# Copies of values bound behind the selections of turned probabilities, in attention followed by a feed-forward block

## The chip, the cores and the metric

The kernel runs on one core of one Trainium2 chip. The metric is the device time of one execution in microseconds (us). Before the change three runs took 711.4, 712.26 and 714.54 us, median 712.26. One more execution was profiled; the rows below are from it.

## The reference

Input are q, k and v of shape 4 x 8 x 768 x 64 (batch, heads, positions, head size), and two weights, 512 x 2048 and 2048 x 512. All is fp32.

```
scores = q @ k^T / sqrt(64)
keep   = (key < 4) or (0 <= query - key < 128)        # sinks, or a sliding window
a      = softmax over the kept keys
x      = (a @ v), heads side by side: 3072 x 512
h      = x @ w_in                                      # 3072 x 2048
g      = h * erf(softplus(h))
out    = g @ w_out                                     # 3072 x 512
```

## The kernel before

The 3072 positions are worked on in 12 groups of 256. Attention goes in 48 steps (s = 0 to 47): a step is one pair of heads of one group, so four steps make a group. The feed-forward block goes through each group in 16 blocks of 128 hidden units, taken in pairs; a pair bears the number m of its first block (h_54 is a hidden pair, g_55 its activations).

A step s from 15 on runs like this:

- `load` fetches k, q and v of the step into SBUF (DMAs issued by SyncE: L232, L241).
- `prep` turns k and q with a VectorE transpose (L345); `kcopy` (L328) and a small copy (L358) on GpSimd complete the keys, kq.
- `score` multiplies them on TensorE (L404, tile ps); VectorE merges the two window halves and takes the maximum (L417, L422), ScalarE takes the exponential (L426).
- `norm` divides by the sums on VectorE (L433 to L456). `ptrans` transposes in blocks (L469, L470) and writes the result to DRAM (L472); `pread` reads it back so that the probabilities are turned (L498, tile pa).
- `phalf` and `halves` run on GpSimd. Copies make the tile pz (L509, L513), then four selections at L522 keep one triangle each: two write pz from pa, and the last two write pa in place.
- `dup` copies the values v of the step into the tile vz, in two halves (L321 and L323), on GpSimd too.
- `av`, on TensorE (L563), multiplies pa with v and pz with vz. It needs the last selection of the step, and both copies. `xfin` (L582, L583) splits the result into a high and a low part for the feed-forward block.

In `core`, the av of step s - 2 stands just ahead of the scores of step s on TensorE. The feed-forward block uses L771 for the hidden products (24 matmuls of 256 columns a pair), ScalarE and VectorE for the activation (L784 to L793), L800 on VectorE for the high half of g and L801 on GpSimd for its low half, and L816 to L818 for the projection (12 matmuls of 512 columns a pair).

What sets the order. The program gives its pieces out in rounds (`plan`, `attn`), each with a priority (`at`, table `O`). A scheduler then sets the instructions of each engine in an order by these priorities and by when it expects their inputs; each engine runs its list strictly in that order. `follow(prev, ins)` binds an instruction behind another without a semaphore. In the plan `phalf(s - 1)` is given out one round ahead of `dup(s)`:

```
plan.setdefault(pos(s) + 5, []).append(("phalf", phalf, s))
plan.setdefault(pos(s) + 2, []).append(("dup", dup, s))      # pos(s) = 4 s - 12
```

but nothing binds the two, and `dup(s)` only needs its values to have landed, so the scheduler sets it where GpSimd would otherwise wait.

Of the kernel before, what the change touches and what calls it, by code (L numbers as in the profile page):

```python
# [45 lines left out]
TT = 15  # L46
# [16 lines left out]
def kernel(  # L63
# [11 lines left out]
    nc = tc.nc  # L75
# [62 lines left out]
    def fast_path():  # L138
        with ExitStack() as st:
# [52 lines left out]
            vz = pers.tile([P, 2, 2, H, D], F32, name="vz")  # L192
# [10 lines left out]
            mark = {}  # L203
# [3 lines left out]
            lo, hi = slice(0, HP), slice(HP, P)  # L207
# [109 lines left out]
            def dup(s):  # L317

                g, c = divmod(s, NPAIR)
                t, cs = stp[s]["v"], slice(2 * c, 2 * c + 2)  # L320
                nc.gpsimd.tensor_copy(vz[lo, 0, :, cs], t[lo, 1:])  # L321
                x = t[hi, 1:2].broadcast_to([HP, 2, 2, D]) if g % GPB == 0 else t[hi, :2]
                nc.gpsimd.tensor_copy(vz[hi, 1, :, cs], x)  # L323

            def kcopy(s):

# [3 lines left out]
            def follow(prev, ins):  # L330

                if prev is not None:
                    tc.add_manual_dep(
                        ins.ins, prev.ins.name,
                        mybir.DependencyInfo(mybir.DependencyClass.NoSync, mybir.DependencyReason.DATA), reason="order",
                    )
                return ins
# [123 lines left out]
            def ptrans(s):  # L461
# [27 lines left out]
                if i0:  # L489
                    nc.scalar.copy(pz[lo, :, 0, lo], tp[lo, :, 0, lo])  # L490
                halves(pa, pz, i0)

            def pread(s, last):
# [7 lines left out]
            def phalf(s):  # L501

                d = stp[s]
                pa, pz = d["pa"], work.tile([P, 2, 2, P], F32, tag="pz", bufs=AL, name=f"pz_{s}")
                d["pz"] = pz
                i0 = int(g_of(s) % GPB == 0)
                if i0:
                    nc.gpsimd.memset(pz[hi, :, 0, hi], 0.0)
                    nc.gpsimd.tensor_copy(pz[lo, :, 0, lo], pa[lo, :, 0, lo])  # L509
                for hf in (lo, hi):  # L510
                    other = hi if hf == lo else lo
                    y = d["pa5"][hf, 4, other].rearrange("p (a b t) -> p a b t", a=1, b=1)
                    nc.gpsimd.tensor_copy(pz[hf, :, :, other], y.broadcast_to([HP, 2, 2, HP]))  # L513
                halves(pa, pz, i0)

            def halves(pa, pz, i0):

                for hf in (lo, hi):
                    x = pa[hf, :, i0:, hf]
                    old, new = (1, ALU.is_gt), (-1, ALU.is_ge)  # L520
                    for out, (sg, op) in zip((pz[hf, :, i0:, hf], x), (new, old) if hf == lo else (old, new)):
                        nc.gpsimd.affine_select(  # L522
                            out=out, in_=x, pattern=[[0, 2], [0, 2 - i0], [-sg, HP]], compare_op=op, fill=0.0, base=0,
                            channel_multiplier=sg,
                        )
# [64 lines left out]
            def pos(s):  # L590

                return s if s < NE else 3 * s - 6 if s < 2 * NPAIR else 4 * s - 12

            plan = {}
            for s in range(NSTEP + AL):
                if s < NSTEP:
                    for what, fn, a in (
                        ("prep", prep, max(4, s - 1) if NE <= s < 2 * NPAIR else pos(s) - 3), ("norm", norm, pos(s) + 1 + (s == 1)), ("ptrans", ptrans, pos(s) + 2),
                        ("load", load, pos(s) - 4),
                    ):  # L600
                        if what == "load":
                            if s < 2 * NPAIR:
                                continue
                            plan.setdefault(a, []).append(("load", load_v, s))
                            a -= 1
                            if s >= TT + 2:
                                plan.setdefault(a - 2, []).append(("load", lambda s: load(s, "k"), s))
                                fn = load_q
                        plan.setdefault(max(a, 0 if what == "prep" else -1), []).append((what, fn, s))
                    if s >= TT:  # L610
                        if s + 2 >= NSTEP:
                            plan.setdefault(pos(s) + 3, []).append(("pread", lambda s: pread(s, mark["d", s]), s))
                        plan.setdefault(pos(s) + 5, []).append(("phalf", phalf, s))
                    if s >= 2 * NPAIR:
                        plan.setdefault(pos(s) + 2, []).append(("dup", dup, s))
                    if s // NPAIR % GPB < GPB - 1:
                        plan.setdefault(pos(s) + (2 if s < NE else 1), []).append(("kcopy", kcopy, s))
                plan.setdefault(pos(s), []).append(("core", core, s))
                if s < 2 * NPAIR:
                    x = pos(s) + (3 if s < NE else 5)  # L620
# [22 lines left out]
            for n in range(32):  # L643
                x = n - 16
# [326 lines left out]
```

## Time and profile before

| | before |
|---|---|
| median of 3 runs | 712.26 us |
| profiled execution | 710.78 us, its span 708.8 us |
| granted TensorE clock | 0.992 of full speed |
| busy: TensorE, its weight loads | 681.0 us (96%), 564.1 us |
| busy: VectorE, ScalarE, GpSimd | 550.0, 494.0, 297.8 us |
| TensorE idle for GpSimd (L522; L801) | 5.2 us in 6 places; 1.5 us in 4 |
| GpSimd idle for values (L321) | 21.5 us in 12 places |

The span is the time from the first to the last instruction that the profile shows; the execution's own time lies 2 us above it. Busy times overlap between engines, so they don't add up to the span. An idle time stands with the instruction that ended it and with what it waited for.

### The profile page before, as it was taken

Reading aid. Unit: us, or ns where it says so; the run is one execution under the profiler, and the core shown is the slowest. Engines: PE = TensorE matmul, PEld = TensorE weight load, DVE = VectorE, ACT = ScalarE, POOL = GpSimd, SP = SyncE. Lnnn points to the kernel's source line nnn. Section 1 sums busy time; section 2 is a strip of 40 time slices with the busy share of each in tenths; the row PEclk is TensorE's granted clock in tenths of the full one; section 3 lists DMA queues with packets and bytes.
Section 4 is the critical chain, followed back from the end, with each engine's and each line's share of the span. In section 5 each row is a group of like instructions: output and inputs, shape, how many; then the busy total and the mean of one; then the engine's idle time right before and its main releaser. Section 6 shows DMA issues by size and latency. Waiting matters only on the chain. (4 is left out here: it accounts for less than half of the span.)

```text
span 708.8 us, 16156 instructions
## 1 busy us (share of the span) xinstructions
PE 681.0 (96%) x5515; PEld 564.1 (80%) x5515; DVE 550.0 (78%) x1473; ACT 494.0 (70%) x1157; POOL 297.8 (42%) x501
## 2 busy tenths in 40 slices
PE   6789999999999999899999999999999999999997
PEld 3566566687888888788788888888888888889895
DVE  6979998787889889788898588788798687754352
ACT  4777777986984867476677586686578567586572
POOL 3512410234445545554555455455464337342221
PEclk9989999999999999999999999999999999999999
DMA  7999410202216454653564354453553543220001
GB/s 174 296 325 318 177 31 17 63 16 50 63 35 121 108 113 94 139 102 73 123 119 83 71 122 82 99 120 75 119 103 78 101 95 71 44 68 1 30 1 35
DMA packets 246858, 70.10 MB, mean 99 GB/s; under 512 B 214704, under 2 KB 238896, under 8 KB 246768
## 3 DMA queue, kind: packets, MB, share of 16 engines
q1 hardware_dynamic: 246208, 68.92, 41.8%
q8 instruction: 46, 0.75, 0.4%
q14 instruction: 44, 0.36, 0.2%
q10 hardware_dynamic: 560, 0.07, 0.1%
HBM read 50.27 MB, written 18.42 MB: 97 GB/s over the span
## 5 line engine op out<-in xcount | busy, mean ns | idle before, releaser
L771 PE MATMUL h<-xh,wt 128*128 128x256 f32 x1408 | 271.2, 283 | 1.2 <-DVE u L793 1.2
L771 PEld LDWEIGHTS h<-xh,wt 128*128 128x128 f32 x1408 | 223.4, 188 | 15.6 <-issue 7.8
L771 PE MATMUL h<-xl,wt 128*128 128x256 f32 x704 | 197.0, 280 | 0.3 <-DVE xl L583 0.3
L801 POOL TENSOR_TENSOR g<-u,g 128x512 fp32r<-128x512 f32 x84 | 113.6, 1353 | 176.4 <-DVE g L800 161.5
L789 ACT ACTIVATE u<-r 128x512 f32<-128x512 f32 x288 | 163.3, 623 | 20.4 <-DMA out_dram<-ot 5.5
L793 DVE SCALAR_TENSOR_TENSOR u<-u,u 128x512 f32<-128x512 f32 x168 | 136.2, 811 | 14.5 <-ACT u L789 1.4
L771 PEld LDWEIGHTS h<-xl,wt 128*128 128x128 f32 x704 | 132.4, 188 | 7.0 <-issue 2.8
L816 PE MATMUL o<-wt,g 128*128 128x512 f32 x336 | 133.2, 396 | 0.7 <-DVE g L800 0.6
L817 PE MATMUL o<-wt,g 128*128 128x512 f32 x336 | 132.2, 393 | 0.0
L818 PE MATMUL o<-wt,g 128*128 128x512 f32 x336 | 129.4, 396 | 1.7 <-POOL g L801 1.5
L426 ACT ACTIVATE pst<-pst,neg 128x144 f32<-128x144 f32 x192 | 77.4, 405 | 65.3 <-DVE neg L422 65.2
L793 DVE SCALAR_TENSOR_TENSOR u<-u,h 128x512 f32<-128x512 f32 x84 | 56.7, 675 | 50.6 <-ACT u L789 46.3
L784 ACT ACTIVATE r<-h 128x512 f32<-128x512 f32 x96 | 56.9, 593 | 45.3 <-PE h L771 34.4
L522 POOL TENSOR_SCALAR_AFFINE_SELECT pz<-pa 64x256 f32<-64x256 f32 (+1 forms) x96 | 47.5, 495 | 67.3 <-ACT pa L484 66.0
L816 PEld LDWEIGHTS o<-wt,g 128*128 128x128 f32 x336 | 63.1, 188 | 14.5 <-ACT u L789 1.3
L818 PEld LDWEIGHTS o<-wt,g 128*128 128x128 f32 x336 | 61.8, 188 | 15.9 <-POOL g L801 3.0
L817 PEld LDWEIGHTS o<-wt,g 128*128 128x128 f32 x336 | 63.1, 188 | 10.3 <-issue 0.3
L786 ACT ACTIVATE r<-r 128x512 f32<-128x512 f32 x96 | 60.6, 631 | 2.7
L785 ACT ACTIVATE r<-r 128x512 f32<-128x512 f32 x96 | 60.6, 632 | 2.5
L800 DVE CAST g<-u 128x512 fp32r<-128x512 f32 x84 | 37.5, 447 | 25.0 <-PE o L818 21.5
L513 POOL COPY pz<-pa 64x256 f32<-64x256 f32 x66 | 31.9, 484 | 56.3 <-DMA pa<-pd 55.5
L522 POOL TENSOR_SCALAR_AFFINE_SELECT pa<-pa 64x256 f32<-64x256 f32 (+1 forms) x96 | 47.7, 497 | 4.9
(99 smaller groups left out, 915.1 us busy)
## 6 DMA issues: line engine op xcount, KB each, us to landing
pd<-turn SPq DMA_DIRECT2D x33, 320.0 KB, 2.6
pa<-pd SPq DMA_DIRECT2D x132, 80.0 KB, 2.6
ws<-in_moe_w_in_dram SPq DMA_DIRECT2D x16, 512.0 KB, 6.0
ws<-in_moe_w_out_dram SPq DMA_DIRECT2D x16, 512.0 KB, 8.6
out_dram<-ot SPq DMA_DIRECT2D x24, 256.0 KB, 2.4
v<-in_v_dram SPq DMA_DIRECT2D x56, 96.0 KB, 2.5
kq<-in_k_dram SPq DMA_DIRECT2D x144, 32.0 KB, 2.0
kq<-in_q_dram SPq DMA_DIRECT2D x144, 32.0 KB, 2.2
```

The lines of the kernel that those rows point to most:

```text
L426: mark["e", s] = nc.scalar.activation(y, y, AF.Exp, bias=d["neg"][:, i, h : h + 1], scale=-1.0, accum_out=d["sum"][:, i, h : h + 1])
L522: nc.gpsimd.affine_select(out=out, in_=x, pattern=[[0, 2], [0, 2 - i0], [-sg, HP]], compare_op=op, fill=0.0, base=0, channel_multiplier=sg,)
L771: last = nc.tensor.matmul(o, wt[NC * j + c][:, p, fs], xt[e][:, c, :], start=(m == 0), stop=(m == len(ops) - 1))
L784: nc.scalar.activation(r, h, AF.Tanh, bias=b_t, scale=0.5)
L785: nc.scalar.activation(r, r, AF.Square, bias=b_v, scale=-0.5)
L786: nc.scalar.activation(r, r, AF.Square, bias=b_r)
L789: sq = nc.scalar.activation(u, r, AF.Square, bias=b_a[i], scale=CS)
L793: pr = nc.vector.scalar_tensor_tensor(out=acc, in0=u, scalar=CC[i] * CS**2, in1=x, op0=ALU.add, op1=ALU.mult)
L801: nc.gpsimd.tensor_tensor(gl, acc, gh.bitcast(F32), op=ALU.subtract)
L816: behind(nc.tensor.matmul(o, gh[:, ws], wt[16 + f][:, 0, :], start=(f == 0), stop=False))
L817: nc.tensor.matmul(o, gh[:, ws], wt[16 + f][:, 1, :], start=False, stop=False)
L818: nc.tensor.matmul(o, gl[:, ws], wt[16 + f][:, 0, :], start=False, stop=(f == NF - 1))
```

## The change

Two lines bind the copies of `dup`, for steps over TT = 15, behind `mark["half"]`, and `halves` puts its latest selection there. When `dup(s)` is given out, the latest `halves` is that of step s - 1, so the copies of step s stand behind the last selection of step s - 1 on GpSimd. The bond is of the order alone: no instruction and no semaphore wait is added.

```
 def dup(s):
     g, c = divmod(s, NPAIR)
     t, cs = stp[s]["v"], slice(2 * c, 2 * c + 2)
-    nc.gpsimd.tensor_copy(vz[lo, 0, :, cs], t[lo, 1:])
+    behind = mark["half"] if s > TT else None
+    follow(behind, nc.gpsimd.tensor_copy(vz[lo, 0, :, cs], t[lo, 1:]))
     x = t[hi, 1:2].broadcast_to([HP, 2, 2, D]) if g % GPB == 0 else t[hi, :2]
-    nc.gpsimd.tensor_copy(vz[hi, 1, :, cs], x)
+    follow(behind, nc.gpsimd.tensor_copy(vz[hi, 1, :, cs], x))
...
 def halves(pa, pz, i0):
...
-            nc.gpsimd.affine_select(
+            mark["half"] = nc.gpsimd.affine_select(
                 out=out, in_=x, pattern=[[0, 2], [0, 2 - i0], [-sg, HP]], compare_op=op, fill=0.0, base=0,
```

Lines from 322 on have a number higher by one in the changed kernel (L522 is L523, L321 is L322). The scheduler makes a new order of every engine. GpSimd, at the selections of step 22; the number after a tile's name is the step, v_24 are the values of step 24. Before:

```order
L522 AFFINE_SELECT pz_22_3878<-pa_22_3740 64x4x64
L513 COPY pz_22_3878<-pa_22_3740 64x4x64
L522 AFFINE_SELECT pz_22_3878<-pa_22_3740 64x4x64
L522 AFFINE_SELECT pa_22_3740<-pa_22_3740 64x4x64
L321 COPY vz_131<-v_24_3846 64x2x128
L323 COPY vz_131<-v_24_3846 64x2x128
L522 AFFINE_SELECT pa_22_3740<-pa_22_3740 64x4x64
L358 COPY kq_130<-kq_130 128x3x16
```

And in the changed kernel:

```order
L523 AFFINE_SELECT pz_22_3878<-pa_22_3740 64x4x64
L514 COPY pz_22_3878<-pa_22_3740 64x4x64
L523 AFFINE_SELECT pz_22_3878<-pa_22_3740 64x4x64
L523 AFFINE_SELECT pa_22_3740<-pa_22_3740 64x4x64 x2
L322 COPY vz_131<-v_23_3654 64x2x128
L324 COPY vz_131<-v_23_3654 64x2x128
L359 COPY kq_130<-kq_130 128x3x16
```

The two selections of pa now stand together, and the copies behind them are those of step 23, not 24.

TensorE, around av of step 17. Before, the hidden pair h_54 (24 matmuls, just above this piece), the 12 projections of g_49 and four of g_51 stand ahead of it; o_3 are the outputs of group 3:

```order
L816 MATMUL o_3_0_3008<-wt_17_2026,g_49_2862 128x512
L817 MATMUL o_3_0_3008<-wt_17_2026,g_49_2862 128x512
L818 MATMUL o_3_0_3008<-wt_17_2026,g_49_2862 128x512
L816 MATMUL o_3_1_3009<-wt_17_2026,g_49_2862 128x512
L817 MATMUL o_3_1_3009<-wt_17_2026,g_49_2862 128x512
L818 MATMUL o_3_1_3009<-wt_17_2026,g_49_2862 128x512
L816 MATMUL o_3_0_3008<-wt_18_2068,g_51_2985 128x512
L817 MATMUL o_3_0_3008<-wt_18_2068,g_51_2985 128x512
L816 MATMUL o_3_1_3009<-wt_18_2068,g_51_2985 128x512
L817 MATMUL o_3_1_3009<-wt_18_2068,g_51_2985 128x512
L563 MATMUL av_17_3071<-pa_17_2798,v_17_2548 64x128 x2
```

In the changed kernel the same av stands right behind the projections of g_47:

```order
L818 MATMUL o_2_1_2276<-wt_31_1975,g_47_2794 128x512
L819 MATMUL o_2_1_2276<-wt_31_1975,g_47_2794 128x512
L564 MATMUL av_17_3071<-pa_17_2798,v_17_2548 64x128 x2
L564 MATMUL av_17_3071<-pa_17_2798,v_17_2548 64x64 x4
L564 MATMUL av_17_3071<-pz_17_2946,vz_131 64x64 x8
L405 MATMUL ps_19_3088<-kq_130 64x208 x2
L405 MATMUL ps_19_3088<-kq_130 64x224 x2
L405 MATMUL ps_19_3088<-kq_130 64x208 x2
L405 MATMUL ps_19_3088<-kq_130 64x224 x2
L817 MATMUL o_3_0_3008<-wt_16_2023,g_49_2862 128x512
L818 MATMUL o_3_0_3008<-wt_16_2023,g_49_2862 128x512
L819 MATMUL o_3_0_3008<-wt_16_2023,g_49_2862 128x512
```

The projections of g_49 and h_54 have moved behind av and the scores of step 19.

The same count of feed-forward matmuls that change sides was made for the other steps: ahead of av of step 16, 11 projections of g_47 have moved behind; ahead of the scores of step 17, four of g_45; ahead of av of step 18, 33 hidden products and 8 projections, taken from where it stood before. From step 24 on av stands where it stood, or later: by up to two hidden pairs and two dozen projections at step 43.

## Rows read from the trace of the kernel before

**Rows 1.** The page, busy time of each engine (share of the span) and instructions.

```profile
PE 681.0 (96%) x5515; PEld 564.1 (80%) x5515; DVE 550.0 (78%) x1473; ACT 494.0 (70%) x1157; POOL 297.8 (42%) x501
```

**Rows 2.** Stages: window, us, busy time of each engine, clock, DMA.

```profile
0.00:50.00 50.00, 37.14 (x290) 25.84 (x291) 39.87 (x146) 33.18 (x100) 18.45 (x40) 0.92 0.93 256
...
400.00:450.00 50.00, 50.00 (x433) 43.65 (x430) 41.88 (x115) 36.87 (x86) 23.97 (x35) 1.00 0.46 97
```

**Rows 3.** Waits of TensorE, whole span: us in total, times, longest.

```profile
PE av L563 <- POOL pa L522: 5.2, 6, 1.9
...
PE o L818 <- POOL g L801: 1.5, 4, 0.6
PE h L771 <- DVE u L793: 1.2, 3, 0.5
```

**Rows 4.** Timeline of TensorE, instructions it idled before: start, us, instruction, [idle].

```profile
280.57 0.67 PE L563 MATMUL av<-pa,v 128*64 128x128 f32 x12 [0.24 <-POOL pa L522]
292.95 0.74 PE L818 MATMUL o<-wt,g 128*128 128x512 f32 x2 [0.56 <-POOL g L801]
301.95 0.67 PE L563 MATMUL av<-pa,v 128*64 128x128 f32 x12 [1.95 <-POOL pa L522]
...
352.73 0.34 PE L563 MATMUL av<-pa,v 128*64 128x64 f32 x4 [1.03 <-POOL pa L522]
```

**Rows 5.** Timeline of GpSimd, selections of step 22 and copies between them.

```profile
299.51 0.42 POOL L522 TENSOR_SCALAR_AFFINE_SELECT pa<-pa 64x256 f32<-64x256 f32 x1
299.88 0.84 POOL L321 COPY vz<-v 64x256 f32<-64x256 f32 x1
300.76 0.77 POOL L323 COPY vz<-v 64x256 f32<-64x256 f32 x1
301.48 0.42 POOL L522 TENSOR_SCALAR_AFFINE_SELECT pa<-pa 64x256 f32<-64x256 f32 x1
```

**Rows 6.** Timeline of GpSimd, copies and last selections of steps 17 and 18.

```profile
241.85 0.39 POOL L321 COPY vz<-v 64x256 f32<-64x256 f32 x1
242.28 0.77 POOL L323 COPY vz<-v 64x256 f32<-64x256 f32 x1
243.01 0.60 POOL L522 TENSOR_SCALAR_AFFINE_SELECT pa<-pa 64x256 f32<-64x256 f32 x1
...
255.43 0.39 POOL L321 COPY vz<-v 64x256 f32<-64x256 f32 x1
...
256.21 0.42 POOL L522 TENSOR_SCALAR_AFFINE_SELECT pa<-pa 64x256 f32<-64x256 f32 x1
```

**Rows 7.** Timeline of TensorE: 18 projections, hidden products, av of steps 17 and 18.

```profile
231.58 0.39 PE L816 MATMUL o<-wt,g 128*128 128x512 f32 x1
...
235.47 0.40 PE L818 MATMUL o<-wt,g 128*128 128x512 f32 x1
...
238.00 0.28 PE L771 MATMUL h<-xl,wt 128*128 128x256 f32 x1
...
243.23 0.28 PE L771 MATMUL h<-xh,wt 128*128 128x256 f32 x1
...
247.10 0.67 PE L563 MATMUL av<-pa,v 128*64 128x128 f32 x12
...
257.76 0.67 PE L563 MATMUL av<-pa,v 128*64 128x128 f32 x12
```

**Rows 8.** Timeline of VectorE beside the copies of step 22.

```profile
299.64 1.63 DVE L793 SCALAR_TENSOR_TENSOR u<-u,u 128x512 f32<-128x512 f32 x2
```

**Rows 9.** Idle time of GpSimd before L321: until what, us, times.

```profile
  DMA v<-in_v_dram: 21.5, 12
```

**Rows 10.** Timelines of GpSimd and TensorE, last selection and av of step 30.

```profile
397.99 0.42 POOL L522 TENSOR_SCALAR_AFFINE_SELECT pa<-pa 64x256 f32<-64x256 f32 x1
...
405.51 0.67 PE L563 MATMUL av<-pa,v 128*64 128x128 f32 x12
```

More of the change, by code (lines that the diff above doesn't have):

```diff
@@ L320, in dup @@
                 t, cs = stp[s]["v"], slice(2 * c, 2 * c + 2)
-                nc.gpsimd.tensor_copy(vz[lo, 0, :, cs], t[lo, 1:])
+                behind = mark["half"] if s > TT else None
+                follow(behind, nc.gpsimd.tensor_copy(vz[lo, 0, :, cs], t[lo, 1:]))
                 x = t[hi, 1:2].broadcast_to([HP, 2, 2, D]) if g % GPB == 0 else t[hi, :2]
-                nc.gpsimd.tensor_copy(vz[hi, 1, :, cs], x)
+                follow(behind, nc.gpsimd.tensor_copy(vz[hi, 1, :, cs], x))
             def kcopy(s):
@@ L521, in halves @@
                     for out, (sg, op) in zip((pz[hf, :, i0:, hf], x), (new, old) if hf == lo else (old, new)):
-                        nc.gpsimd.affine_select(
+                        mark["half"] = nc.gpsimd.affine_select(
                             out=out, in_=x, pattern=[[0, 2], [0, 2 - i0], [-sg, HP]], compare_op=op, fill=0.0, base=0,
```

## The prediction, made before the changed kernel was run

> **What bounds the kernel now.** I read the page first, then the table by stage, then TensorE's waits, then the timelines of TensorE and GpSimd around those waits. The page puts TensorE at 681.0 us of the 708.8 us span; GpSimd, which the change touches, is busy for 297.8 [rows 1]. So an instruction of GpSimd costs time only where TensorE waits for it. By stage TensorE is idle for 12.9 us in the first 50 us, before any moved copy, and not at all from 400 to 450 [rows 2]. What TensorE owes to GpSimd is small: the products of probabilities and values (I call them av, with the step's number) waited 5.2 us in 6 places for the selections of turned probabilities at L522, and the projections 1.5 us in 4 places for the low halves of L801; 1.2 us went to VectorE [rows 3]. The timeline shows which of these lie where the change acts: 0.24 us before av of step 20, 0.56 us at a projection at 292.95, 1.95 us before av of step 22, and 1.03 us before av of step 26 [rows 4]. (Steps are told apart by counting the copies of L321, which are those of steps 8 to 47 in turn, against the order of instructions.)
>
> **What the change does, and what it costs.** No work is added or removed: the 32 steps from 16 on still make two copies each. In before, the copies for step s+2 stand between the two last selections of step s. Step 22 shows the price: one selection, two copies of 0.84 and 0.77 us, and only then the other selection, at 301.48, which ends at 301.90; av of step 22 starts 0.05 us later after its 1.95 us of idling [rows 4, 5]. Without the copies that selection could have run from 299.88: it comes 1.60 us earlier. At step 17 the same subtraction gives 243.01 - 241.85 = 1.16 us, at step 18 256.21 - 255.43 = 0.78 us [rows 6].
>
> The copies now belong to the next step instead of the one after it and come some ten us later. Three things could suffer. The av that reads them: it starts at 257.76 for step 18, while the copies for step 18 would end about a microsecond after 243.61, so they are over ten us early [rows 6, 7]. What stands behind them on GpSimd, mostly one L801 and one or two copies of keys: those were behind the same copies and both selections before, so mostly nothing is later for them. Their own load: 12 copies waited 21.5 us for values to land [rows 9]; a step later they find them there. I take nothing for this, since TensorE's list has no wait for a copy of values [rows 3]; if it freed GpSimd wherever it waited, the most it could give back on TensorE is still the 1.5 us of L801 [rows 3].
>
> The larger part is not in the diff. The scheduler expects the selections earlier, and so sets the av and the following scores of steps 16 to 23 ahead of feed-forward work. I price this with two spacings: 18 projections in a row start 0.229 us apart (3.89 us over 17), the products of the hidden layer 0.114 us apart (5.23 us over 46) [rows 7]. Ahead of av of step 17, 24 hidden products and 16 projections go behind it: 24 x 0.114 + 16 x 0.229 = 6.40 us. For step 18 it is 33 hidden products and 8 projections: 5.59 us; counted the same way, 4.8, 5.3, 4.8 and 2.75 us for steps 19 to 22. The scores move too, which pulls the probabilities along: by 0.92 us for step 17 (four projections), 2.52 for step 18 (eleven), then 6.4, 5.6, 4.8 and 5.3.
>
> Now the slack. At step 17 the last selection ends at 243.61 and av starts at 247.10: 3.49 us. TensorE arrives 6.40 us earlier, the selection 1.16 us (copies gone) plus 0.92 us (scores earlier): 6.40 - 3.49 - 1.16 - 0.92 = 0.83 us of new waiting. At step 18 the slack is 257.76 - 256.63 = 1.13 us; of the 5.59 us, 0.83 are already lost, and 4.76 - 1.13 - 0.78 - 2.52 = 0.33 us are waited [rows 6, 7]. Together 1.16 us. From step 19 on the scores are pulled at least as far as av is, or nearly, so the selection arrives in time: at step 22 TensorE would arrive at 301.95 - 1.95 - 0.56 - 0.24 - 2.75 + 1.16 = 297.61, and the selection ends at 301.90 - 1.60 - (0.24 + 5.3 - 1.16) = 295.92, 1.7 us before. So the waits of 0.24 and 1.95 us go. The 0.56 us goes too, because the projection that had it now stands behind 24 more hidden products (2.7 us) and an av. The 1.03 us at step 26 stays: around its selections the order of GpSimd and the place of av are as before.
>
> Sum: -0.24 - 0.56 - 1.95 + 0.83 + 0.33 = -1.59 us. The profiled execution took 710.78 us (span 708.8), so it would take 709.2; the median of before is 712.26, 1.5 us above it, and with the same subtraction I predict 710.7 us. The bounds: no new wait and all the old ones of [rows 4] gone is -3.78; and nothing on the other engines following TensorE is +2.75 (worked out below).
>
> From step 27 on av moves later or stays, by up to 11 us, and scores with it. The tightest place that I find is av of step 30, which stays while its scores come 5.5 us later. In before its selection ends at 398.41 and av starts at 405.51 [rows 10], 7.10 us, so 1.6 us are left and I take zero; the cover gone, it would cost what it is short.
>
> Contention bears on the size. The copies of step 22 took 0.84 us where those of step 18 took 0.39 [rows 5, 6], and beside them VectorE ran two L793, each on two tensors u [rows 8]. The Trainium skill, page "SBUF — State Buffer", section "Who interferes with whom", says that GpSimd and VectorE share one pair of ports, and that a VectorE instruction with two inputs in SBUF and a GpSimd instruction that reads SBUF exclude each other for the length of the one that came first. The trace agrees in this place. By that rule the selection that takes the copies' place meets the same VectorE work and is itself doubled: 0.42 us less is won at each of steps 17, 18 and 22. Step 22 has 1.7 us to spare; at the other two it adds 0.84 us of waiting, and the sum would be -0.75 us, 711.5 instead of 710.7.
>
> **The rivals.** (1) The probabilities don't follow. TensorE's order is pulled forward, but phalf's selections of steps 17 to 22 end at the same clock time as before, because the chain score, exponential, transposes, two transfers sets them and not GpSimd's queue. Then TensorE idles at av of steps 17 to 20 until it is where it was; by step 22 the order has given 2.5 us back to the feed-forward work, its old waits of 2.75 us are filled with work, and what remains is the 2.75 us by which av of step 22 was pulled: 715.0 us. For it: slack at step 18 was 1.13 us and at step 20 none [rows 4, 6, 7]. Against it: the scores are themselves set ahead. It decides as soon as the wait at step 17 is over 2 us. Beside it, the activation of one hidden pair now stands behind the normalisation of step 18 on VectorE; if a projection is late by up to 1 us there, 716.
> (2) More goes than I count: no new wait, and besides the three waits also the 1.03 us at step 26 and the 1.2 us for VectorE [rows 3, 4], which the new order happens to pull apart: 2.75 + 1.03 + 1.2 = 4.98 us, 707.3 us. For it: some thirty pairs of copies leave the path, not three. Against it: TensorE has no idle time to give back from 400 to 450 [rows 2], and nothing in the change touches step 26.
> (3) Nothing measurable: what leaves av returns as waits for transfers or for L801 of the same size: 712.3 us.
> That the order isn't changed as the words say is no rival: the order of GpSimd shows it.
>
> **How the numbers follow.** Forecast 0.55 (709.0 to 712.3); rival (1) 0.17; (2) 0.15; (3) 0.13. Half a per cent, 3.6 us, is about what a measurement can tell from no change: below 708.7 is faster, above 715.8 slower. Faster: most of (2) and a little of the forecast's low end, 0.16. Slower: the upper half of (1) with its late projection, and later steps falling short, 0.12. The rest, 0.72, is no change. The range reaches from just above (2) to a little beyond (1), 707.6 to 715.6, since the runs of before alone spread from 711.4 to 714.54.
>
> **What would show it.** Right: GpSimd's timeline has two L522 writing pa next to each other and then the two copies, without a wait for the load of values; the waits of 0.24 and 1.95 us are gone, and TensorE waits about 1 us for L522 or the pa transfer between 235 and 260 us. Wrong for the step on slack: that wait is zero or above 2 us. Wrong for the step on step 22: av there still waits over 0.5 us. Wrong altogether: TensorE's idle time changes by over 4 us, or its busy time does.

## The result, and the profile after

Five runs of the changed kernel took 703.3 to 705.77 us, median 704.2, beside 712.01 for the kernel before on the same chip: ratio 0.9879 (95% interval 0.986 to 0.9897). Forecast were 710.7 us and a range from 707.6: the gain is 7.8 us and not 1.6. The profiled execution took 705.77 us with a span of 704.1.

The page, busy time of each engine, against [rows 1]:

```profile
PE 677.9 (96%) x5515; PEld 563.8 (80%) x5515; DVE 550.4 (78%) x1473; ACT 495.0 (70%) x1157; POOL 296.9 (42%) x501
```

No engine has fewer instructions; what went is mostly TensorE's waiting. The page books it only in part: of the 4.7 us that the span is shorter, 3.1 stand as busy time of TensorE and 1.6 as idle time, since the modelled ends of matmuls hide part of a wait (below). TensorE's waits from 200 to 300 us, which answer to [rows 3] (line, releaser, us in total, times, longest). From 300 to 600 us the same view is empty: the 1.2 us for VectorE and the wait at step 26 are gone too.

```profile
PE av L564 <- POOL pa L523: 1.8, 1, 1.8
PE o L819 <- POOL g L802: 0.7, 1, 0.7
```

TensorE at av of steps 17, 22 and 26, which answers to [rows 4, 7] (start, us, instruction, idle time before it):

```profile
242.52 0.67 PE L564 MATMUL av<-pa,v 128*64 128x128 f32 x12 [1.80 <-POOL pa L523]
...
299.06 0.33 PE L564 MATMUL av<-pa,v 128*64 128x128 f32 x2
...
351.37 0.44 PE L564 MATMUL av<-pa,v 128*64 128x128 f32 x4
```

GpSimd at the selections of steps 17 and 22, against [rows 5, 6]:

```profile
238.93 0.39 POOL L514 COPY pz<-pa 64x256 f32<-64x256 f32 x1 [1.71 <-DMA pa<-pd]
...
241.57 0.90 POOL L523 TENSOR_SCALAR_AFFINE_SELECT pa<-pa 64x256 f32<-64x256 f32 x2
242.53 0.39 POOL L322 COPY vz<-v 64x256 f32<-64x256 f32 x1
242.96 0.77 POOL L324 COPY vz<-v 64x256 f32<-64x256 f32 x1
...
297.85 0.96 POOL L523 TENSOR_SCALAR_AFFINE_SELECT pa<-pa 64x256 f32<-64x256 f32 x2
298.88 0.47 POOL L322 COPY vz<-v 64x256 f32<-64x256 f32 x1
```

The two selections stand together, the copies follow. GpSimd's idle time for values to land has fallen from 21.5 us [rows 9] to the line below; all of it lies before the moved copies, which wait for no values any more:

```profile
  DMA v<-in_v_dram: 11.7, 5
```

**Where the time went.** I measured two stretches of TensorE that hold the same instructions in both kernels: "early", from the end of h_40 to the end of h_96 (194.9 to 389.5 us in before), and "late", from the end of h_128 to the end of the projections of g_159 (495.1 to 619.9). Before they last 194.62 and 124.76 us. In a second profiled execution of the changed kernel (e8_after_again) they last 191.28 and 121.42: 3.34 us less in each, together 6.7 us, where the medians timed side by side with e8 differ by 6.9. In the first one the early stretch lasts 193.39: 1.6 of the 2.1 us more are a lower clock of TensorE (last section), and 0.3 a longer wait of a projection at 221 us.

A stall I also read by spacing: the start of an instruction less the start of the one before it, less what that pair takes elsewhere (0.229 us from projection to projection). The idle time in a row is smaller, because the modelled end of a matmul overlaps the next: 1.95 us is 2.01 by spacing, 0.56 is 0.72, 1.03 is 1.20. In the late stretch before had stalls of 0.66, 0.61, 0.24, 0.45 and 0.32 us, 2.28 together. So they are not all of the 3.34: right behind each of them one more start comes 0.08 to 0.11 us late, 0.5 us together, which goes with them, and the other 0.6 us no single row shows. The idle times at two of the five:

```profile
519.99 0.36 PE L771 MATMUL h<-xh,wt 128*128 128x256 f32 x1 [0.49 <-DVE u L793]
...
579.29 0.38 PE L771 MATMUL h<-xh,wt 128*128 128x256 f32 x1 [0.44 <-DVE u L793]
```

### The profile page after: what moved, and what is told of

Its sections match the earlier page's. It is cut to its first block, busy times and chain, and to the rows that moved or that the text cites. A ratio compares the mean times of both kernels' runs of the same rounds, so it can differ in the third digit from the quotient of the medians.

```text
span 704.1 us, 16145 instructions
## 1 busy us (share of the span) xinstructions
PE 677.9 (96%) x5515; PEld 563.8 (80%) x5515; DVE 550.4 (78%) x1473; ACT 495.0 (70%) x1157; POOL 296.9 (42%) x501
## 5 line engine op out<-in xcount | busy, mean ns | idle before, releaser
L794 DVE SCALAR_TENSOR_TENSOR u<-u,u 128x512 f32<-128x512 f32 x168 | 130.4, 776 | 14.3 <-ACT u L790 2.0
L523 POOL TENSOR_SCALAR_AFFINE_SELECT pz<-pa 64x256 f32<-64x256 f32 (+1 forms) x96 | 49.9, 520 | 66.1 <-ACT pa L485 65.0
L514 POOL COPY pz<-pa 64x256 f32<-64x256 f32 x66 | 30.1, 456 | 56.0 <-DMA pa<-pd 54.8
L442 DVE TENSOR_SCALAR pst<-pst,sum 128x128 f32<-128x128 f32 x168 | 51.7, 371 | 1.4
```

What stands on the lines that cost most here:

```text
L442: nc.vector.tensor_scalar_mul(p, p, sm[:, i, h : h + 1])
L794: pr = nc.vector.scalar_tensor_tensor(out=acc, in0=u, scalar=CC[i] * CS**2, in1=x, op0=ALU.add, op1=ALU.mult)
```

## The experiments

Each was timed in several rounds beside before on the same chip; the stretches are from one profiled execution each. In a kernel called bound, every engine's instructions are chained in a given order by bonds of order alone, as in `follow`.

| run | median us | ratio to before (95%) | early us | late us |
|---|---|---|---|---|
| before | 711.2 to 712.2 | 1 | 194.62 | 124.76 |
| e1_pool_alone | 727.49 | 1.0199 to 1.026 | 206.07 | 129.96 |
| e2_rest_alone | 738.67 | 1.0323 to 1.0389 | 200.57 | 146.80 |
| e3_early_steps | 707.47 | 0.991 to 0.9959 | 191.59 | 124.98 |
| e4_late_steps | 707.45 | 0.9918 to 0.9961 | 194.74 | 121.42 |
| e5_short_copies | 709.6 | 0.9967 to 0.9997 | 193.59 | 124.51 |
| e6_from_20 | 707.53 | 0.9934 to 0.9964 | 194.81 | 121.42 |
| e7_late_order | 711.88 | 0.9996 to 1.0025 | 194.89 | 124.64 |
| e8_after_again | 704.32 | 0.9881 to 0.9918 | 191.28 | 121.42 |
| e9_pool_late | 712.09 | 1.0 to 1.0025 | 195.75 | 124.47 |
| e10_late_both | 714.84 | 1.0012 to 1.005 | 196.04 | 126.12 |
| e11_av17_later | 704.54 | 0.9887 to 0.9915 | 192.24 | 121.42 |
| e12_from_40 | 709.37 | 0.9935 to 0.9971 | 194.93 | 122.20 |
| e13_from_42 | 710.42 | 0.9964 to 0.9991 | 194.36 | 123.43 |
| e14_order_only | 708.15 | 0.9913 to 0.9956 | 194.63 | 121.42 |

Seven executions with before's early order (before, e4, e7, e9, e10, e12, e13) put the early stretch at 194.36 to 196.04: that is its scatter, though 1.6 us of the longest, that of e10, are a lower clock (last section). The six with the changed kernel's late order and a late stretch without a wait all show 121.42.

**Order of GpSimd alone, order of the rest alone.** Bound: GpSimd in the changed kernel's order and the others in before's (e1), and the reverse (e2).

> GpSimd runs its list in the order of the changed kernel; TensorE, VectorE, ScalarE and SyncE are bound to the order of before (all instructions the same). Theory Q (the gain is GpSimd's own: the selections end earlier because the copies left their place): nearly all of it, 704 to 706 us. Theory R (the gain comes from the new order of TensorE and VectorE, which the scheduler made because of the bond): at most the waits that sat behind copies go, 0.3 us at step 20, 2.0 at step 22 and perhaps 1.3 at step 26, so 708.5 to 711 us, and the waits of TensorE for VectorE's activations near 520 and 580 to 591 us stay.

> The reverse: GpSimd is bound to the order of before (copies between the two last selections), the other four engines to the order of the changed kernel. Theory Q: no gain, 711 us or more, with TensorE waiting 3 us or more at the products of step 17, which stand 6.4 us earlier than before. Theory R: most of the gain stays, 707 us or less, and the waits near 520 and 580 to 591 us are gone.

Both are slower than either kernel, by 15 and 27 us against before, so neither Q nor R is right. TensorE's waits of e1, then of e2, from 200 to 660 us:

```profile
PE o L899 <- POOL g L882: 9.4, 4, 4.0
PE av L643 <- POOL pa L602: 4.7, 3, 3.4
```

```profile
PE o L896 <- POOL g L879: 17.3, 6, 6.1
PE av L640 <- POOL pa L599: 8.9, 4, 5.2
```

In both the low halves of the activations stand behind work on probabilities that is not due yet on the other engines. The order of GpSimd and that of the others fit each other and can't be exchanged as a whole; no theory of one engine alone survives this. Part of the loss is a lower clock behind the longest waits (last section).

**Early steps, late steps.** The bond for steps 16 to 25 alone (e3), for 26 to 47 alone (e4).

```
-                behind = mark["half"] if s > TT else None
+                behind = mark["half"] if TT < s < 26 else None     # e3
+                behind = mark["half"] if s > 25 else None          # e4
```

> The bond holds for steps 16 to 25 only; the order is that of the changed kernel up to there and that of before afterwards. In the two traces the place where both orders meet again (hidden pair h_80 at 335.6 us) was reached 0.1 us later in the changed kernel: by that the early part gives nothing, 711.5 to 712.5 us. If the slow stretch of TensorE after its new wait at step 17 (granted clock 0.97 from 200 to 250 us) belongs to that execution alone, the early part gives up to 2.5 us more: 709.5. My prediction's sum (1.6 us) would be 710.4.

> The bond holds for steps 26 to 47 only. The traces of before and after drift by 5.0 us between 335 us and the end, so: 707 us, with no wait for L522 left at step 26 if that wait is of the late part, or with it (1.0 us idle) if it went because of the early part; then 708.3. If the late gain needs the early part, 710 or more. If the two parts add up, the gains of this kernel and of the one with steps 16 to 25 sum to 7.8 us.

Each gives about 4.5 us by the medians (e3 comes out below all three times that were expected of it), with intervals of 3 to 6 us, together not distinguishable from the 7.8 of the whole. By the stretches each gives its own half: e3 is 3.0 us shorter early and not late, e4 3.34 late and not early. So the gain has two parts, and the late one, which I had put at zero, is as large as the early one.

**The copies themselves.** Bound to before's order; the copies shrink to 4 of every 64 elements, so most of the values are left out.

```
+                n = 4 if s > TT else D
-                nc.gpsimd.tensor_copy(vz[lo, 0, :, cs], t[lo, 1:])
+                nc.gpsimd.tensor_copy(vz[lo, 0, :, cs, :n], t[lo, 1:, :, :n])
...
```

> All five engines are bound to the order of before; the two copies of values of every step from 16 on write 4 of every 64 elements (most of the values are left out, so its output is not the reference's). Theory A (the copies cost what they take in GpSimd's queue, ahead of the selection that av waits for): the waits for L522 at steps 20, 22 and 26 shrink from 0.24, 1.95 and 1.03 us to under 0.5 us together, the stretch from step 40 to 46 keeps its length of 124.8 us (end of the hidden pair 128 to end of the projections of g_159), and the time is 709.3 to 710.3 against 712.0. Theory B (what matters is the order that the scheduler makes of all engines): the waits stay above 2 us together, 711.5 to 712.5. Theory C (the copies beside VectorE slow its work down everywhere): the stretch from step 40 to 46 shortens by over 1.5 us too, 707.5 to 708.5.

Theory A by its time, 709.6 us, not by its waits. Those of 0.24 us at step 20 and of 0.56 at the projection are gone, and the early stretch is 1.0 us shorter, the late one hardly. At step 22 av still waits 1.86 us, at step 26 0.76. At step 22 TensorE comes a microsecond earlier, and the selections on both sides of the small copies take twice their 0.42 us, each beside a VectorE instruction that reads two tensors u (the later one is shown):

```profile
300.73 0.44 PE L644 MATMUL av<-pa,v 128*64 128x128 f32 x4 [1.86 <-POOL pa L603]
```

```profile
298.57 0.90 POOL L603 TENSOR_SCALAR_AFFINE_SELECT pa<-pa 64x256 f32<-64x256 f32 x1
299.43 0.19 POOL L402 COPY vz<-v 64x16 f32<-64x16 f32 x1
299.66 0.19 POOL L404 COPY vz<-v 64x16 f32<-64x16 f32 x1
299.80 0.87 POOL L603 TENSOR_SCALAR_AFFINE_SELECT pa<-pa 64x256 f32<-64x256 f32 x1
```

```profile
299.69 0.71 DVE L875 SCALAR_TENSOR_TENSOR u<-u,u 128x512 f32<-128x512 f32 x1 [0.50 <-ACT u L871]
```

Copies that cost next to nothing are worth about a microsecond in the old order; the interval of the ratio is wide, 0.2 to 2.3 us.

**Order without the copies' place.** Bound to the changed kernel's order, but on GpSimd the two copies of each step from 17 on stand between the last two selections of the step before.

> All engines bound to the order of the changed kernel, but on GpSimd the two copies of each step from 17 on stand between the last two selections of the step before, as they did for another step in before. Theory A (the order of the other engines makes most of the gain, and the copies ahead of the selection cost only where av waits for it, at step 17, by 0.8 to 1.6 us): the wait at step 17 is 2.6 to 3.4 us, no other wait for L523 above 0.5 us, the late stretch 121.4 to 121.8 us, time 705.0 to 706.3 against 704.3 of the changed kernel. Rival (it is the copies' place that counts, and the orders only fit it): waits at three places or more, 707 to 711 us.

The time, 708.15 us, and the number of waits are the rival's; the late stretch is theory A's. Late, the copies' place is worth nothing: 121.42 us with them among the selections again. Early all that the order had won is gone, 194.63 us against 191.28. TensorE's waits:

```profile
PE o L895 <- POOL g L878: 2.4, 2, 1.7
PE av L639 <- POOL pa L598: 1.6, 3, 1.1
```

But the copies' place is not shown to be the cause. By spacing the three waits before av are 1.79 us together, and the one of the changed kernel is 1.87. What is new is 0.89 us at a hidden pair at 258.86 and 1.87 at a projection at 267.94, for a low half that stands behind selections of step 19. Both go back to ScalarE, which stands still for 3.64 us before one activation; VectorE waits for it, and the norm of step 19 and the hidden pair's u stand behind that on VectorE:

```profile
253.12 0.63 ACT L866 ACTIVATE u<-r 128x512 f32<-128x512 f32 x1 [3.64 <-DMA out_dram<-ot]
```

In the kernel the tiles u take turns in four buffers with the output tiles ot. Here this u waits until an output has been written (issued at 250.69, landed at 253.09). In e8 the same instruction runs at 249.35, without that wait, and the turned probabilities of step 19 reach GpSimd at 260.57 and not at 264.19. So e14 differs from the changed kernel in more than the place of the copies. Without the two stalls its early stretch would be 191.9 us (an estimate, 194.63 - 0.89 - 1.87), close to e8's 191.28.

So early the short way for the copies alone gives 1.0 us (e5) and everything together 3.3; what the order of the other engines gives without the copies' place stays open.

**What the late part is.** First theory: before, hidden pairs stand behind the norm of a step on VectorE and behind its exponentials on ScalarE. Bound to before's order, with these instructions moved:

```
DVE  first L793 of h_132   ahead of the scaling of step 40
DVE  first L793 of h_150   ahead of the turning of step 44
DVE  L800 of g_151, L793 x3 of h_152   ahead of the norm of step 45
ACT  L784, L785, L786, L789 x3 of h_152   ahead of the exponentials of step 45
```

> All five engines are bound to the order of before, with 11 instructions moved in it: on VectorE the first L793 of h_132 ahead of the scaling of step 40, the first L793 of h_150 ahead of the turning of step 44, L800 of g_151 and the three L793 of h_152 ahead of the norm of step 45; on ScalarE the six activations of h_152 ahead of the exponentials of step 45. The copies stay as in before. Theory A (the late gain is that hidden pairs no longer stand behind the norm of a step on VectorE and ScalarE): TensorE's stalls at 519.99, 579.29, 586.51, 587.99 and 591.21 us (0.66, 0.61, 0.24, 0.44, 0.32 by spacing, 2.27 together) go, the stretch from the end of h_128 to the end of the projections of g_159 falls from 124.8 to 122.3 to 122.8 us, and the time is 709.5 to 710.2 against 712.0. Theory B (the late gain needs GpSimd's copies out of the way): the stretch stays at 124.3 to 125, the time within 0.5 us of before. Theory C (the steps 44 and 45, later now, hold up av instead): a wait for L522 of 0.5 us or more between 595 and 615 us, and the time as before or 1 us longer.

All five stalls went, and the stretch stayed at 124.64: new ones of 0.15, 0.42, 1.32 and 0.40 us, 2.29 together, came for the 2.28. The longest is for the low half of an activation; GpSimd's timeline shows it in front of the probabilities of step 44, for which it idles 8 us, with two low halves behind them in its list:

```profile
590.44 0.74 PE L899 MATMUL o<-wt,g 128*128 128x512 f32 x2 [1.16 <-POOL g L882]
```

```profile
584.53 0.39 POOL L593 COPY pz<-pa 64x256 f32<-64x256 f32 x1 [8.02 <-DMA pa<-pd]
...
589.12 1.26 POOL L882 TENSOR_TENSOR g<-u,g 128x512 fp32r<-128x512 f32 x1
```

Theory A named the stalls, not what stood right behind them. The stretch is theory B's, but two copies of values, 0.9 us, are only part of what stands ahead of that low half, and e14 shows their place worth nothing late in the changed order. Theory C's wait for L522 did not come. So I moved the low halves of g_131, g_151 and g_153 ahead of that work (e9), and then did both (e10).

> All engines bound to the order of before, with three low halves moved on GpSimd: L801 of g_131 ahead of the first copy from the probabilities of step 39, L801 of g_151 ahead of the first copy of step 44, L801 of g_153 ahead of the first selection of pa of step 44. The copies of values stay. Theory A (the late gain needs both: low halves ahead of work that waits for probabilities on GpSimd, and hidden pairs ahead of a step's norm on VectorE and ScalarE; alone each only hands the wait on): the stalls of 0.66, 0.61 and 0.44 us at the hidden pairs stay, the stretch from the end of h_128 to the end of the projections of g_159 falls from 124.76 to 124.2 to 124.6 us, the time by 0.1 to 0.6 us. Rival (GpSimd's list alone makes the late gain): stretch 121.4 to 122.5 us, time 2.3 to 3.4 us below before.

> The moves of e9_pool_late and those of e7_late_order together, and L800 of g_153 ahead of the norm of step 45 as well; the copies stay. Theory A (both together make the late gain, without any copy moved): the waits for L801 at 522.76 (0.42) and 590.44 (1.32) of e7_late_order go, and none of the five of before comes back; the stretch falls from 124.76 to 121.4 to 122.3 us, the time by 2.3 to 3.3 us against before. Rival (the gain belongs to the copies of steps 39 and 44 that stood among the selections, or to the place of av of step 43, and no order of the rest gives it): the stretch stays above 124 us.

e9: the stretch, 124.47, is as theory A has it, but its stalls are two, of 1.69 and 0.44 us at hidden pairs, and the time is not below before. e10: theory A falls, with a stretch of 126.12 us; 1.7 of them are a lower clock from 594 us on (last section), and 124.4 would still be before's. The low halves are in time, and the norm of step 45, now later, stands ahead of the next hidden pair on VectorE:

```profile
594.02 0.36 PE L852 MATMUL h<-xh,wt 128*128 128x256 f32 x1 [2.21 <-DVE u L874]
```

In all three orders some feed-forward work still stands behind that of steps 44 and 45. In all of them, as in before, TensorE gives out the scores of the two steps 8.6 us apart; in the changed kernel they are 20.2 us apart. The first two rows are before's, the last two the changed kernel's:

```profile
565.85 0.99 PE L404 MATMUL ps<-kq 64*64 64x208 f32 x16
574.46 0.99 PE L404 MATMUL ps<-kq 64*64 64x208 f32 x16
...
563.01 0.99 PE L405 MATMUL ps<-kq 64*64 64x208 f32 x16
583.16 0.99 PE L405 MATMUL ps<-kq 64*64 64x208 f32 x16
```

Two bonds tell whether that is it: `s > 39` moves av of step 43 and the scores of step 45 behind three and a half hidden pairs, as in the changed kernel; `s > 41` leaves them behind one.

> The bond for steps 40 to 47 only. The scheduler then sets av of step 43 and the scores of step 45 behind three and a half hidden pairs that follow the scores of step 44, as in the changed kernel, instead of behind one; up to step 39 the order is that of before. Theory A (the late gain is this place: two steps' scores no longer 8.6 us apart, so VectorE and ScalarE get through the norms and the hidden pairs between them): the stretch from the end of h_128 to the end of the projections of g_159 falls from 124.76 to 121.4 to 122.2 us, time 2.5 to 3.4 us below before. Rival (the gain needs the bonds of the earlier steps): stretch above 123.5 us, time 0 to 1.3 us below before.

> The bond for steps 42 to 47 only. Here the scheduler leaves av of step 43 and the scores of step 45 where before has them, behind one hidden pair; av of step 44 comes two pairs earlier. Theory A: the stalls at the hidden pairs stay, the stretch is 124 to 126 us, the time 0.8 us below to 1 us above before. Rival (the copies of the last steps out from between the selections are the gain, wherever av of step 43 stands): stretch 121.4 to 122.5 us, time 2.3 to 3.4 us below before.

e12: theory A, 122.20 us. What it lacks to 121.42 is the first stall, which belongs to step 40 and has not gone:

```profile
521.86 0.36 PE L772 MATMUL h<-xh,wt 128*128 128x256 f32 x1 [0.64 <-DVE u L794]
```

e13 lies between theory A and its rival: 123.43. The stalls at the hidden pairs near 579 and 588 us are gone here too, and av of step 44, which comes two pairs earlier, waits:

```profile
586.41 0.67 PE L564 MATMUL av<-pa,v 128*64 128x128 f32 x12 [0.40 <-POOL pa L523]
```

So TensorE's order from step 40 on, all engines following, makes 2.56 of the 3.34 us with only eight steps bound. The place of av of step 43, and with it the distance of the scores of steps 44 and 45, is not all of it: 1.33 come without it, with the scores 8.6 us apart as before. How the gain divides between the moves of that order stays open.

**A better version?** The wait of step 17 looked avoidable, by a later start of the bond (`s > 19`, e6) or by putting av of step 17 behind eight projections in the bound changed kernel (e11).

> The bond for steps 20 to 47 only, the rest as in the changed kernel. Theory A (the bond pulls av of steps 17 and 18 too far forward, and the wait of 1.3 to 1.8 us at step 17 is the price): no wait for L523 above 0.5 us between 235 and 260 us, all else as in the changed kernel, 702.0 to 703.3 us, or 1 to 2 us below the changed kernel in the same call. Rival (what is not pulled forward at steps 16 to 19 is met later: the wait for step 20 or 22 comes back with 1 to 2 us): 704 to 706 us.

> The changed kernel, all engines bound to its order, but on TensorE av of step 17 and the scores of step 19 stand behind eight projections of g_49 (8 x 0.229 = 1.83 us) instead of ahead of them. Theory A (the wait of 1.8 us at step 17 is only av being set too early, and the work behind it is ready): the wait falls to 0.2 us or less, nothing else comes, 702.2 to 703.0 us, 1.3 to 1.9 below the changed kernel's 704.3. Rival (scores of step 19 come later by up to 1 us and av of step 19 or 20 waits for it, or what comes after step 26 takes it back as it did for the step 17 wait of the early bond): 703.5 to 704.5 us.

Neither gains. e6 misses both theories and loses the whole early part: by spacing stalls of 0.56, 1.43 and 1.69 us at av of steps 18, 20 and 22. e11 ends at the upper edge of its rival's range, by other waits than that names: in e11 the wait before av of step 17 is gone; 0.6 us of idling stand at av of step 18 and 1.5 at a projection instead, so the time is the changed kernel's:

```profile
264.80 0.73 PE L896 MATMUL o<-wt,g 128*128 128x512 f32 x2 [1.52 <-POOL g L879]
```

No version beat the changed kernel.

**The changed kernel again.**

> The changed kernel once more. If the slow stretch behind the wait of step 17 (243.9 to 247.1 us, granted clock 0.97 from 200 to 250) belongs to the wait, it is there again: clock below 0.98 in 200 to 250, the place of av of step 20 about 2.4 us earlier than before. If it was an accident of that one execution: clock 1.00 there, av of step 20 some 4.4 us earlier, as with the bond of the early steps alone. The time is 703.3 to 705.8 in both cases.

704.32 us. The wait of 1.80 us is there again, the low clock is not: so the wait does not always bring it.

## Why the prediction was wrong

**The step that failed: "From step 27 on ... I take zero."** It measured 3.34 us (e4, and the late stretch of every run with that order). The one slack that I worked out there was right: 1.6 us forecast for step 30, 1.47 measured (its last selection ends at 402.66):

```profile
404.13 0.55 PE L564 MATMUL av<-pa,v 128*64 128x128 f32 x8
```

I asked only whether something new would be late. Against rival (2) I cited one stage without idle time, 400 to 450 us [rows 2]; the 1.2 us of waits for VectorE [rows 3] lay in the next hundreds of microseconds, in the order that "moves later or stays". There, the later order was the gain: from step 40 on alone it gives 2.56 us (e12), and 1.33 with av of step 43 left in its place (e13).

None of my signs of being wrong was met in the profiled execution: the wait at step 17 is under 2 us, av of step 22 does not wait, and TensorE's idle and busy time on the page changed by 1.6 and 3.1 us, each under the 4 that I had set. (In e8 the busy time changed by 4.7.) No sign of mine looked behind step 26.

**"The 1.03 us at step 26 stays": wrong**, 1.20 us by spacing went. No copies stood among its selections. All of step 26 came earlier: its probabilities reached GpSimd at 346.27 and not 348.44 us, and the last selection ended at 350.36 and not 352.67. This belongs to the bond of the early steps (e3 has it, e4 not); what made the probabilities earlier was not tested by itself.

**The removed waits, 0.24 + 0.56 + 1.95: right**, and larger by spacing (0.31, 0.72, 2.01). At step 22 the forecast had TensorE 1.7 us behind the selection; it is 0.24 (298.82 to 299.06), and 1.33 in e8, which was enough.

**The new waits.** Step 17: 0.83 forecast, 1.80 measured. Arrival was right: TensorE came 6.38 us earlier (6.40). The selection came 1.14 earlier, what the copies alone were to give (1.16). The term of 0.92 for earlier scores failed: they start 1.00 us earlier, at 225.68 and not 226.68, but the first copy from their probabilities only 0.15 (238.93 against 239.08), and the copy from the second half not at all (240.74 against 240.65). VectorE still has other work, so it starts merging the scores only 0.54 us earlier; the norm behind it takes longer (its four scalings 1.18 us against 1.02), and the probabilities go out to DRAM 0.20 us earlier (233.03 against 233.23). The merging and the first copy, before, then the merging in the changed kernel:

```profile
227.72 0.90 DVE L417 COPY_PREDICATED ps<-tri,ps 64x256 f32<-64x256 int8 x2
...
239.08 1.13 POOL L513 COPY pz<-pa 64x256 f32<-64x256 f32 x1 [1.24 <-DMA pa<-pd]
```

```profile
227.18 0.89 DVE L418 COPY_PREDICATED ps<-tri,ps 64x256 f32<-64x256 int8 x2
```

Without that term the same sum gives 6.40 - 3.49 - 1.16 = 1.75. Step 18: 0.33 forecast, none measured; the selection there is 4.3 us earlier and has 3.25 us to spare (1.47 in e8, where TensorE is not slowed by its clock).

**The early sum.** -1.59 forecast, -3.34 in e8. By spacing 0.31 + 0.72 + 2.01 + 1.20 = 4.24 went and 1.87 came, -2.37; 0.14 is a stall ahead of the change that was shorter; the other 0.8 us no row singles out.

**Contention.** By the Trainium skill ("SBUF — State Buffer", "Who interferes with whom") the prediction had the selections that take the copies' place doubled. In the changed kernel they are not: two took 0.90 us at step 17 and 0.96 at step 22, since its order has other VectorE work beside them: one u and the hidden products h, which lie in PSUM, at step 17 (241.90 us), scalings of one tensor at step 22 (297.69). In e5, with VectorE's old order, they are: 0.90 and 0.87 us each. What the Trainium skill says there of two inputs in SBUF agrees with these rows; what was wrong was to take the old neighbours for the new ones.

**The rivals.** Rival (1) gave "the wait at step 17 is over 2 us" as its point; at 1.80 it stayed below. Rival (2), more goes than counted, held in its direction and named both waits, at 707.3 us, 3 us short: it took the waits at their idle rows, and counted only waits.

## What to carry to other kernels

A bond of two copies made the scheduler reorder all five engines, and half of the gain lay some 250 us behind the waits that I had priced: with such a scheduler, price every stage where the bounding engine waits, also for engines that the change does not name. Read a stall from the spacing of starts, and expect that removing one wait at an engine that serves several streams in order hands it to the next in line: here five stalls came back, as long, at other instructions, until TensorE's own order changed too. And when engines are bound to a recorded order, see that their tiles also share buffers as they did: in e14 one did not, and 2.8 us came of it.

## What the runs showed of the hardware

After the wait of 1.80 us TensorE ran slower for 3.5 us in the first profiled execution, and not in the second, after the same wait. The windows (us, busy time of engines, granted clock, DMA) of the first, then of the second:

```profile
242.00:248.00 6.00, 5.48 (x52) 4.11 (x53) 5.05 (x16) 4.55 (x10) 3.67 (x5) 0.72 0.67 150
```

```profile
242.00:248.00 6.00, 4.98 (x58) 4.04 (x59) 4.84 (x15) 4.56 (x9) 3.58 (x7) 1.00 0.64 150
```

The scores behind it took 1.70 us against 0.99, and projections started 0.43 us apart instead of 0.23:

```profile
245.81 0.63 PE L818 MATMUL o<-wt,g 128*128 128x512 f32 x1
246.24 0.63 PE L819 MATMUL o<-wt,g 128*128 128x512 f32 x1
246.67 0.61 PE L817 MATMUL o<-wt,g 128*128 128x512 f32 x1
```

A mean of 0.72 over the window fits a stretch at the lower of the two levels (1.2 GHz) and the rest at the upper (2.4 GHz). It cost 1.6 us: from the start of av of step 17 to the sixth projection behind its scores it takes 4.83 us here and 3.25 in e8.

In e10 the lower clock follows two waits, while longer ones in e4, e7, e9 and e12 (2.44 to 2.86 us) are not followed by it: behind the 2.33 us at av of step 22 (302.83 us) the clock is 0.53 from 304 to 306 us, and behind the 2.21 at a hidden pair (594.02) 0.56 and then 0.59 from 594 to 598, with hidden products 0.21 us apart instead of 0.11. Each cost 1.6 to 1.7 us against the same instructions in before.

```profile
304.00:306.00 2.00, 2.00 (x20) 1.35 (x21) 1.55 (x7) 1.92 (x4) 1.00 (x1) 0.53 0.27 64
...
594.00:596.00 2.00, 1.98 (x10) 2.00 (x11) 1.90 (x3) 1.22 (x3) 0.00 (x0) 0.56 0.80 199
```

Over all runs, between 194 and 660 us: no idling under 1.8 us was followed by the lower clock; of those of 1.8 to 2.9 us one in the changed kernel, two in e10 and one in e2 (2.58 us) were, and those in before, e4, e5, e7, e8, e9 and e12 were not; all seven of 3.4 to 6.1 us, in e1 and e2, were. So in the middle range the length of a wait alone does not tell; what does was not tested.
